# Large loads at one point of each twelve steps, masks made sooner, both halves of the maxima in one transposition, lists at every second step: a clustered-attention and mixture-of-experts kernel on one core

## The chip, the cores and the metric

The kernel runs on 1 core of one Trainium2 chip. TensorE multiplies matrices, VectorE (DVE), ScalarE (ACT) and GpSimd (POOL) work on the elements, and SyncE (SP) issues most of the copies (DMA). The metric is the device time of one execution, in microseconds (us); less is better. The time before is 1143.74 us, the median of three runs.

## The reference

Two stages follow each other. First an attention in which a query sees only the keys of its own cluster; then a layer of eight experts, of which each token uses the best two.

```python
# q, k, v: (4, 8, 768, 64); centroids: (8, 16, 64)
q_assign = argmax(einsum(q_n, c_n))          # cluster of each query; the same for k
mask = q_assign[:, :, :, None] == k_assign[:, :, None, :]
scores = where(mask, (q @ k.T) / sqrt(64), -1e9)
attn = softmax(scores, axis=-1)              # with 1e-9 added to the sum
x = (attn @ v), heads side by side           # (3072, 512)

noisy_logits = x @ w_gate + log1p(exp(x @ w_noise)) * noise      # 8 experts
top2, top2_w = the two largest, softmax over the two
for e in range(8):                           # w1: (8, 512, 1024), w2: (8, 1024, 512)
    out[mask] += top2_w * (relu(x[mask] @ w1[e]) @ w2[e])
```

## The kernel before, in words

**Precision.** Numbers are split into a high and a low half, so that the products come out in nearly fp32. `A` and `Bt` are the operands of the scores, three buffers each, used by the pair `p % 3`: high and low halves of q and k, a few rows for the mask (`A[64:80]`) and two rows for the negated row maxima (`Bt[96]`, `Bt[97]`), high and low.

**Steps.** Attention works on 16 pairs of heads (4 batches with 4 pairs each). A pair takes 12 steps, one for each of 2 heads x 6 blocks of 128 keys, so attention has 192 steps, with some in front and four behind. In step `t` the kernel issues, in this order: slot 0; `scores` of step `t`; `split_p` of step `t-1`; slot 1; `values` of step `t-4`; slot 2. Everything else is put into the slots by `at(step, function)`, where the fraction of the step (0, 1/3, 2/3) chooses the slot. The table `AT` holds these places. An engine works its own instructions in the order in which they were issued, and waits in that order; the engines are tied to each other only by what they need from each other. So SyncE, which computes nothing, may run far ahead of or behind the step in which a copy stands.

**What stands in the slots of a pair.** With w = 12(p-2) the preparation of pair p begins two pairs ahead:
- `load_qk` (two copies of 768 KB for four heads; one load in 24 steps) and `load_v` (768 KB, one in 24 steps, a single buffer `vt`, freed by `v_split`);
- `a_split` turns q and k and splits them into `hl`; `b_place` copies `hl` to `A` and `Bt` with ten copies on SyncE (`L434` to `L438`);
- `a_sims`, `a_sum`, `a_max1`, `a_ge`, `a_ky`, `a_max2`, `a_eq` find the cluster of each row on TensorE and VectorE and leave a one-hot `oh` (`L409`); `a_mask` transposes it on TensorE (`L418`) and ScalarE writes `mk`; `b_mask` copies `mk` to `A` with four copies on SyncE;
- `b_max` multiplies the masked scores for the maxima (`L454`), two matmuls a step for twelve steps, and VectorE reduces them (`L457`); it is the first to need the masks, at w + 9.333;
- `b_neg` joins the two halves of a row's maximum in `nm`; `b_negT` transposes `nm` (`L468`), makes the high part on ScalarE and the low part on VectorE, and sends each with a copy to `Bt`; the scores of the pair need them (the second matmul of `L485`).

`scores` makes two tiles a step, each of a matmul on `A` and one on `Bt`, and ScalarE takes their exponential into `pe`. `split_p` makes the low half `pl` of `pe` (`L496`) on GpSimd, for the last pair on VectorE. `values` multiplies high and low halves with v (`L513` to `L519`) and waits for `pl` at `L519`.

**Other work in the slots.** `zero_out` writes 512 KB of zeros to the output, twelve times; `zero_list` fills the table of the experts' tokens. After the last pair of a batch, `store_x` writes the batch's 1.5 MB, `g_logits` to `g_gate` choose the experts, and `g_list` writes the tokens' places into the table: 12 indirect copies a batch on GpSimd, each behind a small memset of `spacer` (`L701`, `L702`). Those of the last batch come after attention. `gather_x` fetches the rows of an expert's tokens; for the first expert's first four tiles it first clears `xg`. `load_w1` and `split_w1` of the first expert stand in the last ten steps.

**Experts.** Each expert has two layers of matmuls (`L952`, `L991`), 832 places an expert.

Of the kernel before, what the change touches and what calls it, by code (L numbers as in the profile page):

```python
# [9 lines left out]
F32 = mybir.dt.float32  # L10
F32R = mybir.dt.float32r
# [3 lines left out]
AF = mybir.ActivationFunctionType  # L15
OP = mybir.AluOpType
# [9 lines left out]
AT = dict(  # L26
    late=1,
    first={'place': -2.333, 'sims': [-3.333, -2.667], 'sum': [-2.333, -2.333], 'max1': -2.333, 'ge': -2.333, 'max2': -2.333, 'eq': -1.333, 'mask': 1.667, 'bmask': 4.0, 'ky': -2.333, 'split': [-5.333, -5.0, -5.333, -4.0], 'bmax': [10.0, 17.0], 'neg': [17.667, 24.667], 'negT': [20.667, 27.667]},
    L=4, qk=-15.667, v=-3.333,
    vscale=-0.667, vsplit=10.667, vstep=1.0, split=[-4.667, -3.667, -4.0, -3.333], place=-0.667,  # L30
    sims=[-3.0, 2.0], sum=[2.333, 3.333], max1=3.333, ge=3.667, max2=4.333, eq=4.667, mask=6.333, bmask=9.0,
    bmax=9.333, neg=20.333, negT=22.0, zero=19.667, zstep=4.333, store=2.667, log=1.667, log2=3.0,
    logstep=0.667, turn=7.667, list=24.0, lstep=1.0, bstep=1.0,
    gate=7.667, gstep=0.333, am=5.333, amstep=0.333, ky=4.0, cut=[13, 20], gplace=17.333,
    vd=[1, 1, 2, 3, 4, 5], sec=-7.333, qf=-13.667,
    fv={'v': -2.333, 'vscale': -1.0, 'am': 0.0, 'amstep': 0.333, 'vsplit': 3.0, 'vstep': 2.0},
    thr=0.333, bsec=0.0)

# [5 lines left out]
class Kernel:  # L44
# [116 lines left out]
    def attention(self, ctx):  # L161
        nc, tc = self.nc, self.tc
# [6 lines left out]
        self.A = [fix.tile([128, 2, 2, S], F32R, name=f"A{i}") for i in range(3)]  # L169
        self.Bt = [fix.tile([128, 2, 2, S], F32R, name=f"B{i}") for i in range(3)]  # L170
        self.oh = [fix.tile([128, 2, 3, 4, 32], BF, name=f"oh{i}") for i in range(2)]
        self.nm = fix.tile([128, 128], F32, name="nm")
        NP = B * H // 2
        self.NP = NP
        self.st = [dict() for _ in range(NP)]
        self.qk, self.vt, self.vv, self.am, self.xt, self.gx = {}, {}, {}, {}, {}, {}
        L = AT["L"]
        sched = {}

        def at(step, f, *a):  # L180
            sched.setdefault(divmod(round(3 * step), 3), []).append((f, a))

        def chain(step, by, fs):
            for i, f in enumerate(fs):
                at(step + by * i, f)


        T = AT
        for p in range(NP):
            b, hp = divmod(p, H // 2)  # L190
            w = 12 * (p - 2)
            if hp == 0:
                for g in range(2):
                    at(w + T["qk"] + 24 * g + (T["qf"] if (b, g) == (0, 1) else 0), self.load_qk, b, g)
                    v = w + 24 * g
                    V = T["fv"] if p + g == 0 else T
                    at(v + V["v"], self.load_v, b, g)
                    for h in range(0, 4, 2):
                        at(v + V["vscale"] + V["amstep"] * h, self.v_max, b, g, h)
                    chain(v + V["am"], V["amstep"], self.v_scale(b, g))  # L200
                    for h in range(4):
                        at(v + V["vsplit"] + V["vstep"] * h, self.v_split, b, g, h)
            P = T["first"] if p == 0 else T
            w += (0, T["sec"], T["thr"])[p] if p < 3 else 0
            for i in range(4):
                at(w + P["split"][i], self.a_split, p, i // 2, i % 2)
            if p == 0:
                at(w + P["sims"][0], self.c_turn)
            at(w + P["place"], self.b_place, p)
            for s in range(2):  # L210
                at(w + P["sims"][s], self.a_sims, p, s)
            for s in range(2):
                at(w + P["sum"][s], self.a_sum, p, s)
            for k, f in (("max1", self.a_max1), ("ge", self.a_ge), ("ky", self.a_ky), ("max2", self.a_max2),
                         ("eq", self.a_eq), ("mask", self.a_mask), ("bmask", self.b_mask)):
                at(w + P[k], f, p)
            if p == 0:
                for s in range(2):
                    for j in range(NJ):
                        at(w + P["bmax"][s] + j, self.b_max, p, s, j)  # L220
                    at(w + P["neg"][s], self.b_neg, p, s, 1)
                    at(w + P["negT"][s], self.b_negT, p, s, 1)
            else:
                w = 12 * (p - 2) + (T["bsec"] if p == 1 else 0)
                for s in range(2):
                    for j in range(NJ):
                        at(w + T["bmax"] + T["bstep"] * (6 * s + j), self.b_max, p, s, j)
                at(w + T["neg"], self.b_neg, p, 0, 2)
                at(w + T["negT"], self.b_negT, p, 0, 2)
            if hp == H // 2 - 1:  # L230
                z = w + 36 + L
                if b + 1 == B:
                    continue
                at(z + T["store"], self.store_x, b)
                for jj in range(NJ):
                    at(z + T["log"] + T["logstep"] * jj, self.g_logits, b, jj)
                    at(z + T["log2"] + T["logstep"] * jj, self.g_logits2, b, jj)
                at(z + T["turn"], self.g_turn, b)
                fs = self.g_gate(b)
                chain(z + T["gate"], T["gstep"], fs[:self.GP])  # L240
                chain(z + T["gplace"], T["gstep"], fs[self.GP:])
                for j in range(2 * NJ):
                    at(z + T["list"] + T["lstep"] * j, self.g_list, b, j)
        at(T["zero"] - 4, self.zero_list)
        for i in range(self.N // 256):
            at(T["zero"] + T["zstep"] * i, self.zero_out, i)
        z = 12 * NP
# [6 lines left out]
            at(z - 7 + i, self.gather_x, 0, i)  # L254
        for i in range(2):
            nc.gpsimd.memset(self.oh[i], 0.0)
        nc.gpsimd.memset(self.nm, 0.0)
        self.fixed_init(0)
        at(-14.4, self.fixed_init, 1)
        at(-8.4, self.fixed_init, 2)  # L260
        self.at = at
        for t in range(min(sched)[0], z + L + 2):
            u = t - L
            slot = lambda i: [f(*a) for f, a in sched.pop((t, i), [])]
# [6 lines left out]
            if 0 <= u < z:  # L271
                p, s, kc = u // 12, (u % 12) // 6, u % 6
# [185 lines left out]

    def b_neg(self, p, s, n):

        W, c = n * self.NJ, self.NJ * s
        self.nc.vector.tensor_tensor(self.nm[:, 0:W], self.aux[:, 500 + c:500 + c + W], self.st[p]["mm"][:, c:c + W],
                                     op=OP.min)

    def b_negT(self, p, s, n):
        nc, W = self.nc, n * self.NJ
        t = self.ps()
        nc.tensor.transpose(t[:, :128], self.nm, self.ident)  # L468
        t = t[:W, :128]
        hi, lo = (self.wk.tile([16, 128], F32R, name=f"nt{i}") for i in range(2))  # L470
        nc.scalar.activation(hi[:W], t, AF.Copy)
        nc.vector.tensor_tensor(lo[:W], t, hi[:W], op=OP.subtract)
        for i, x in enumerate((hi, lo)):
            self.dma(self.Bt[p % 3][96 + i:97 + i, 1, s:s + n], x[:W])


    def scores(self, p, s, kc):
# [11 lines left out]
    def split_p(self, p, s, kc):  # L489

        nc, st = self.nc, self.st[p]
        pe = st["p", s, kc].rearrange("p a n -> p (a n)")
        hi = pe.bitcast(BF).rearrange("p (n two) -> p n two", two=2)[:, :, 1]
        lo = self.wk.tile([128, self.S], F16, name="pl", bufs=5)

        (nc.vector if p == self.NP - 1 else nc.gpsimd).tensor_tensor(lo, pe, hi, op=OP.subtract)  # L496
        st["p", s, kc] = hi, lo

    def values(self, p, s, kc):
# [424 lines left out]
    def gather_x(self, e, t):  # L924
        xg = self.mw.tile([128, self.DM], F32, name="xg", bufs=4)
        r = self.rows(t)
        first = e == 0 and t < self.TA
        n = self.N - self.S if first else self.N
        if first:
            self.nc.gpsimd.memset(xg, 0.0)  # L930
        self.nc.gpsimd.indirect_dma_start(  # L931
            out=xg[:r], out_offset=None, in_=self.xs[:n],
            in_offset=bass.IndirectOffsetOnAxis(ap=self.entry(e, t)[:r, 0:1], axis=0),
            bounds_check=n - 1, oob_is_err=False)
        self.xg[e, t] = xg
# [117 lines left out]
```

## Time and profile before

| what | value |
|---|---|
| runs | 1143.74 us median, 1143.65 to 1147.19 |
| profiled execution | 1145.87 us, of which the span is 1144.0 us |
| busy: TensorE | 1072.6 us, 94% |
| busy: VectorE | 603.8 us, 53% |
| busy: GpSimd | 571.5 us, 50% |
| busy: ScalarE | 479.4 us, 42% |
| HBM | 78.21 MB read, 26.53 MB written |
| TensorE busy, 100 to 500 us | 90.13, 93.76, 95.83, 90.69 us in each 100 us |
| TensorE busy, 700 to 900 us | 200.00 us of 200 us |

The span reaches from the first to the last instruction; the rest of the execution's time lies around it. The first scores start at 50.06 us and attention ends at about 510 us; after that come the experts. "Busy" counts a matmul from its start to its modelled end. In the lists of waits the engine before the arrow waits and the one behind it released it; `ring` is the group of six PSUM buffers that nearly all matmuls write. SPq is SyncE's queue of issued copies.

### The profile page before, as it was taken

Reading aid. Unit: us, or ns where it says so; the run is one execution under the profiler, and the core shown is the slowest. Engines: PE = TensorE matmul, PEld = TensorE weight load, DVE = VectorE, ACT = ScalarE, POOL = GpSimd, SP = SyncE. Lnnn points to the kernel's source line nnn. Section 1 sums busy time; section 2 is a strip of 40 time slices with the busy share of each in tenths; the row PEclk is TensorE's granted clock in tenths of the full one; section 3 lists DMA queues with packets and bytes.
Section 4 is the critical chain, followed back from the end, with each engine's and each line's share of the span. In section 5 each row is a group of like instructions: output and inputs, shape, how many; then the busy total and the mean of one; then the engine's idle time right before and its main releaser. Section 6 shows DMA issues by size and latency. Waiting matters only on the chain. (4 is left out here: it accounts for less than half of the span.)

```text
span 1144.0 us, 22354 instructions
## 1 busy us (share of the span) xinstructions
PE 1072.6 (94%) x8658; PEld 950.4 (83%) x8658; DVE 603.8 (53%) x1298; ACT 479.4 (42%) x961; POOL 571.5 (50%) x619
## 2 busy tenths in 40 slices
PE   4898889999999999989899999999999999999995
PEld 4588787888888888878799889899898898998984
DVE  5876675776688667676145424433344244433411
ACT  3475656666676667564043313223133132231300
POOL 4776664789578957863444323342343233512311
PEclk7899999998999999989899999999999999999998
DMA  8866777664755554122336224432353143423200
GB/s 226 182 151 144 186 179 205 161 152 114 201 120 147 119 147 92 58 91 95 99 95 225 84 72 164 131 109 91 125 171 99 65 150 130 130 86 119 74 31 31
DMA packets 87677, 144.46 MB, mean 126 GB/s; under 512 B 14295, under 2 KB 65879, under 8 KB 87056
## 3 DMA queue, kind: packets, MB, share of 16 engines
q1 hardware_dynamic: 72272, 106.45, 35.0%
q0 software_dynamic: 13712, 36.42, 9.5%
q8 instruction: 69, 1.13, 0.4%
q10 hardware_dynamic: 1584, 0.13, 0.1%
q14 instruction: 40, 0.33, 0.1%
HBM read 78.21 MB, written 26.53 MB: 92 GB/s over the span
## 5 line engine op out<-in xcount | busy, mean ns | idle before, releaser
L496 POOL TENSOR_TENSOR pl<-pe 128x768 f16<-128x768 f32 x180 | 263.3, 1472 | 99.2 <-ACT pe L486 90.3
L952 PE MATMUL ring<-xT,w1t 128*128 128x416 f32 (+2 forms) x1536 | 290.3, 350 | 0.0
L952 PEld LDWEIGHTS ring<-xT,w1t 128*128 128x128 f32 x1536 | 282.7, 188 | 6.6 <-DVE xT L905 0.3
L991 PE MATMUL ring<-w2t,hT 128*128 128x512 f32 x1152 | 273.7, 394 | 0.0
L991 PEld LDWEIGHTS ring<-w2t,hT 128*128 128x128 f32 x1152 | 214.5, 189 | 43.3
L486 ACT ACTIVATE pe<-ring,l 128x384 f32<-128x384 f32 x384 | 202.0, 578 | 93.2 <-PE ring L485 83.6
L1004 POOL DMA_INDIRECT out<-yo,lst x56 | 65.6, 1172 | 236.8 <-DVE yo L1000 187.4
L457 DVE TENSOR_REDUCE aux<-ring 128x1 f32<-128x384 f32 x192 | 107.8, 561 | 94.4 <-PE ring L454 89.9
L485 PE MATMUL ring<-A 128*128 128x384 f32 x384 | 144.3, 376 | 1.0 <-DVE aux L457 0.5
L485 PE MATMUL ring<-B 128*128 128x384 f32 x384 | 132.7, 346 | 4.2 <-DMA B<-nt 4.0
L961 ACT ACTIVATE hT<-ring 128x416 fp32r<-128x416 f32 (+3 forms) x128 | 56.7, 488 | 180.6 <-PE ring L952 168.5
L962 DVE SCALAR_TENSOR_TENSOR hT<-ring,hT 128x416 fp32r<-128x416 f32 (+3 forms) x128 | 66.2, 554 | 123.9 <-ACT hT L961 122.8
L454 PE MATMUL ring<-A 128*128 128x384 f32 x384 | 114.7, 373 | 17.1 <-DMA A<-mk 8.6
L931 POOL DMA_INDIRECT xg<-xs,lst x56 | 65.7, 1173 | 128.5 <-PE ring L942 105.1
L1000 DVE SCALAR_TENSOR_TENSOR yo<-ring,lst,xt 128x512 f32<-128x512 f32 (+1 forms) x49 | 36.7, 750 | 166.6 <-PE ring L991 146.1
L457 DVE TENSOR_REDUCE mm<-ring 128x1 f32<-128x384 f32 x192 | 105.0, 547 | 0.1
L904 ACT ACTIVATE xT<-ring 128x512 fp32r<-128x512 f32 (+1 forms) x56 | 31.0, 566 | 173.1 <-PE ring L942 172.8
L454 PEld LDWEIGHTS ring<-A 128*128 128x128 f32 x384 | 71.5, 197 | 34.6 <-ACT pe L486 14.6
L513 PE MATMUL av<-vv,pe 128*128 128x65 f16 x1152 | 98.9, 196 | 1.1 <-DVE xt L527 1.1
L515 PE MATMUL av<-vv,pe 128*128 128x64 f16 x1152 | 98.0, 194 | 0.0
L513 PEld LDWEIGHTS <-pe 128*128 128x128 bf16 x1152 | 81.7, 100 | 14.8 <-issue 10.9
L485 PEld LDWEIGHTS ring<-B 128*128 128x128 f32 x384 | 74.7, 195 | 6.7 <-issue 4.4
(173 smaller groups left out, 1360.3 us busy)
## 6 DMA issues: line engine op xcount, KB each, us to landing
stg<-in_moe_w SPq DMA_DIRECT2D x64, 512.0 KB
A<-hl SPq DMA_DIRECT2D x30, 384.0 KB
B<-hl SPq DMA_DIRECT2D x30, 384.0 KB
vt<-in_v SPq DMA_DIRECT2D x8, 768.0 KB
out<-zt SPq DMA_DIRECT2D x12, 512.0 KB
xs<-xt SPq DMA_DIRECT2D x4, 1536.0 KB
A<-hl SPq DMA_DIRECT2D x60, 96.0 KB
B<-hl SPq DMA_DIRECT2D x30, 192.0 KB
```

The costliest lines, as they stand in the source:

```text
L454: nc.tensor.matmul(t, A[:, 0, s, j * 128:j * 128 + 128], A[:, 1, s, n * 384:n * 384 + 384], start=True, stop=True)
L457: nc.vector.tensor_reduce(o, t, axis=X, op=OP.max, negate=True)
L485: nc.tensor.matmul(t, M[:, 1 - qi, s, ks], M[:, qi, s, ns], start=not qi, stop=bool(qi))
L486: nc.scalar.activation(pe[:, n], t, AF.Exp, bias=self.l64[:, 0:1], scale=self.scale)
L496: (nc.vector if p == self.NP - 1 else nc.gpsimd).tensor_tensor(lo, pe, hi, op=OP.subtract)
L513: nc.tensor.matmul(av[:, j, :], ph[:, js], vv[:, hh, kj, 64:129], start=(kc == 0 and j == 0), stop=False, skip_group_check=True)
L515: nc.tensor.matmul(av[:, j, :64], ph[:, js], vv[:, hh, kj, 0:64], start=False, stop=False, skip_group_check=True)
L931: self.nc.gpsimd.indirect_dma_start(out=xg[:r], out_offset=None, in_=self.xs[:n], in_offset=bass.IndirectOffsetOnAxis(ap=self.entry(e, t)[ ...
L952: nc.tensor.matmul(p, self.w1t[:, wi, c, f * 128:f * 128 + 128], self.xT[:, xi, c, n0:n1], start=(i == 0), stop=(i == 3 * ND - 1))
L962: nc.vector.scalar_tensor_tensor(h1, x, 0.0, h0, op0=OP.max, op1=OP.subtract)
L991: nc.tensor.matmul(p, self.hT[:, hi, f, t * 128:t * 128 + 128], self.w2t[:, wi, f], start=(i == 0), stop=(i == 3 * NF - 1))
L1004: i = nc.gpsimd.indirect_dma_start(out=self.out, out_offset=bass.IndirectOffsetOnAxis(ap=en[:r, 0:1], axis=0), in_=yo[:r], in_offset=None, ...
```

## The change

- `load_qk` moves from w - 15.667 to w - 20.667 (for the second load at the start, `qf` keeps its place), `load_v` from v - 3.333 to v - 8.667 (the first keeps its place), and `zero_out` from every 4.333 steps from step 19.667 on to every 12 steps from step 27 on. So these copies stand at steps 3 to 3.333 of each twelve. `zero_list` keeps its place (15.667) under a name of its own.
- `a_mask` moves from w + 6.333 to w + 5.667 and `b_mask` from w + 9 to w + 6. The first pair has its own table and keeps its places.
- `b_neg` now makes the low and the high half of the maxima itself, beside each other in `nm`; `b_negT` transposes both at once, with one ScalarE copy and one DMA behind it.
- `g_list` is put at every second step for batches 0 and 1, from step 23 after the batch's mark instead of 24; batch 2 keeps one a step and starts one step sooner.
- From step 5 of the last pair but one, `split_p` is on VectorE (before: only in the last pair).
- The four memsets of `xg` go from GpSimd to VectorE.

```diff
-    L=4, qk=-15.667, v=-3.333,
+    L=4, qk=-20.667, v=-8.667,
 ...
-    sims=..., eq=4.667, mask=6.333, bmask=9.0,
-    bmax=9.333, neg=20.333, negT=22.0, zero=19.667, zstep=4.333, store=2.667, ...
-    logstep=0.667, turn=7.667, list=24.0, lstep=1.0, bstep=1.0,
+    sims=..., eq=4.667, mask=5.667, bmask=6.0,
+    bmax=9.333, neg=20.333, negT=22.0, zero=27.0, zstep=12.0, zlist=15.667, store=2.667, ...
+    logstep=0.667, turn=7.667, list=23.0, lstep=[2.0, 2.0, 1.0], bstep=1.0,
 ...
-    vd=[1, 1, 2, 3, 4, 5], sec=-7.333, qf=-13.667,
+    vd=[1, 1, 2, 3, 4, 5], sec=-7.333, qf=-8.667,
 ...
-                    at(z + T["list"] + T["lstep"] * j, self.g_list, b, j)
-        at(T["zero"] - 4, self.zero_list)
+                    at(z + T["list"] + T["lstep"][b] * j, self.g_list, b, j)
+        at(T["zlist"], self.zero_list)
 ...
     def b_neg(self, p, s, n):
-        W, c = n * self.NJ, self.NJ * s
-        self.nc.vector.tensor_tensor(self.nm[:, 0:W], self.aux[:, 500 + c:500 + c + W], self.st[p]["mm"][:, c:c + W],
-                                     op=OP.min)
+        v, W, c = self.nc.vector, n * self.NJ, self.NJ * s
+        o = self.aux[:, 500 + c:500 + c + W]
+        hi, lo = (self.nm[:, W * i:W * i + W] for i in range(2))
+        v.tensor_tensor(o, o, self.st[p]["mm"][:, c:c + W], op=OP.min)
+        v.tensor_copy(hi, o)
+        v.tensor_tensor(lo, o, hi, op=OP.subtract)
     def b_negT(self, p, s, n):
-        nc, W = self.nc, n * self.NJ
+        nc, W = self.nc, 2 * n * self.NJ
         t = self.ps()
-        nc.tensor.transpose(t[:, :128], self.nm, self.ident)
-        t = t[:W, :128]
-        hi, lo = (self.wk.tile([16, 128], F32R, name=f"nt{i}") for i in range(2))
-        nc.scalar.activation(hi[:W], t, AF.Copy)
-        nc.vector.tensor_tensor(lo[:W], t, hi[:W], op=OP.subtract)
-        for i, x in enumerate((hi, lo)):
-            self.dma(self.Bt[p % 3][96 + i:97 + i, 1, s:s + n], x[:W])
+        nc.tensor.transpose(t[:, :128], self.nm.bitcast(F32), self.ident)
+        nt = self.wk.tile([32, 128], F32R, name="nt")
+        nc.scalar.activation(nt[:W], t[:W, :128], AF.Copy)
+        self.dma(self.Bt[p % 3][96:98, 1, s:s + n], nt[:W])
 ...
-        (nc.vector if p == self.NP - 1 else nc.gpsimd).tensor_tensor(lo, pe, hi, op=OP.subtract)
+        last = p == self.NP - 1 or (p == self.NP - 2 and 6 * s + kc >= 5)
+        (nc.vector if last else nc.gpsimd).tensor_tensor(lo, pe, hi, op=OP.subtract)
 ...
-            self.nc.gpsimd.memset(xg, 0.0)
+            self.nc.vector.memset(xg, 0.0)
```

More of the change, by code (lines that the diff above doesn't have):

```diff
@@ L28 @@
     first={'place': -2.333, 'sims': [-3.333, -2.667], 'sum': [-2.333, -2.333], 'max1': -2.333, 'ge': -2.333, 'max2': -2.333, 'eq': -1.333, 'mask': 1.667, 'bmask': 4.0, 'ky': -2.333, 'split': [-5.333, -5.0, -5.333, -4.0], 'bmax': [10.0, 17.0], 'neg': [17.667, 24.667], 'negT': [20.667, 27.667]},
-    L=4, qk=-15.667, v=-3.333,
+    L=4, qk=-20.667, v=-8.667,
     vscale=-0.667, vsplit=10.667, vstep=1.0, split=[-4.667, -3.667, -4.0, -3.333], place=-0.667,
-    sims=[-3.0, 2.0], sum=[2.333, 3.333], max1=3.333, ge=3.667, max2=4.333, eq=4.667, mask=6.333, bmask=9.0,
-    bmax=9.333, neg=20.333, negT=22.0, zero=19.667, zstep=4.333, store=2.667, log=1.667, log2=3.0,
-    logstep=0.667, turn=7.667, list=24.0, lstep=1.0, bstep=1.0,
+    sims=[-3.0, 2.0], sum=[2.333, 3.333], max1=3.333, ge=3.667, max2=4.333, eq=4.667, mask=5.667, bmask=6.0,
+    bmax=9.333, neg=20.333, negT=22.0, zero=27.0, zstep=12.0, zlist=15.667, store=2.667, log=1.667, log2=3.0,
+    logstep=0.667, turn=7.667, list=23.0, lstep=[2.0, 2.0, 1.0], bstep=1.0,
     gate=7.667, gstep=0.333, am=5.333, amstep=0.333, ky=4.0, cut=[13, 20], gplace=17.333,
-    vd=[1, 1, 2, 3, 4, 5], sec=-7.333, qf=-13.667,
+    vd=[1, 1, 2, 3, 4, 5], sec=-7.333, qf=-8.667,
     fv={'v': -2.333, 'vscale': -1.0, 'am': 0.0, 'amstep': 0.333, 'vsplit': 3.0, 'vstep': 2.0},
@@ L171, in attention @@
         self.oh = [fix.tile([128, 2, 3, 4, 32], BF, name=f"oh{i}") for i in range(2)]
-        self.nm = fix.tile([128, 128], F32, name="nm")
+        self.nm = fix.tile([128, 128], F32R, name="nm")
         NP = B * H // 2
@@ L256, in attention @@
             nc.gpsimd.memset(self.oh[i], 0.0)
-        nc.gpsimd.memset(self.nm, 0.0)
+        nc.gpsimd.memset(self.nm.bitcast(F32), 0.0)
         self.fixed_init(0)
```

## The prediction

> **What bounds the kernel now.** I read the page's first part, then the engine waits of TensorE in the attention stage, then the windows and the timelines around those waits.
>
> ```profile
> span 1144.0 us, 22354 instructions
> PE 1072.6 (94%) x8658; PEld 950.4 (83%) x8658; DVE 603.8 (53%) x1298; ACT 479.4 (42%) x961; POOL 571.5 (50%) x619
> ```
>
> The engine waits of TensorE, 90 to 520 us (columns: total, times, longest):
>
> ```profile
> PE av L519 <- POOL spacer L701: 10.3, 7, 2.3
> PE ring L454 <- DMA A<-mk: 8.6, 4, 3.1
> PE ring L485 <- DMA B<-nt: 3.7, 4, 1.6
> PE ring L454 <- issue: 2.8, 1, 2.8
> ```
>
> TensorE is busy for 94% of the span, so a microsecond in which it stands still in attention is a microsecond of the result; work that other engines lose is not. The waits name three causes. `L519` waits for `pl`, which GpSimd makes late when it also writes the lists (10.3 us). `L454` waits for the masks' copy into `A` (8.6 us in four gaps, and a fifth of 2.8 us that the trace calls "issue" but that lies at the same place). `L485` waits for the maxima in `B` (3.7 us). Together 25.4 us.
>
> TensorE's timeline at three gaps (idle time before the row in brackets), and windows of 10 us:
>
> ```profile
> 130.59 0.96 PE L454 MATMUL ring<-A 128*128 128x384 f32 x2 [3.10 <-DMA A<-mk]
> 271.04 0.51 PE L519 MATMUL av<-vv,pl 128*128 128x65 f16 x6 [2.33 <-POOL spacer L701]
> 388.17 0.35 PE L519 MATMUL av<-vv,pl 128*128 128x65 f16 x6 [2.00 <-POOL spacer L701]
> ```
>
> ```profile
> 100.00:110.00 10.00, 9.93 (x121) 9.17 (x122) 7.96 (x17) 4.52 (x9) 4.88 (x4) 0.83 0.38 78
> 130.00:140.00 10.00, 9.41 (x118) 8.64 (x119) 5.97 (x15) 6.61 (x14) 4.32 (x5) 0.83 0.33 69
> 270.00:280.00 10.00, 8.96 (x76) 8.33 (x77) 3.61 (x8) 5.03 (x9) 9.80 (x9) 0.66 0.34 97
> 390.00:400.00 10.00, 10.00 (x117) 9.75 (x117) 6.05 (x14) 6.85 (x14) 9.75 (x8) 0.83 0.11 20
> 490.00:500.00 10.00, 7.78 (x83) 7.04 (x84) 7.55 (x11) 5.65 (x9) 7.14 (x11) 0.66 0.19 55
> ```
>
> The five windows are those of attention in which the granted clock (third number from the right) drops, and each begins in or just behind a gap of 2 us or more. A mean of 0.83 over 10 us is worth 1.7 us of full-speed work, 0.66 is worth 3.4: up to 11.9 us more hang on the gaps.
>
> The Trainium skill, page "TensorE: Matmul & The Clock Gate", section "HAM oscillation — how this bites in real kernels", sets its limit at idle gaps above about 3.4 us. The trace does not agree: its gap of 2.00 us at 388.17 is followed by a drop. By the page's limit no gap here would cost clock.
>
> **The change part by part.** *Loads and masks.* The masks' copies wait in the one SyncE queue behind the loads, not for their step:
>
> ```profile
> 104.46 2.97 SPq L426 DMA_DIRECT2D A<-hl  x3
> ...
> 115.00 2.69 SPq L555 DMA_DIRECT2D out<-zt  x2
> 117.73 1.58 SPq L293 DMA_DIRECT2D qk<-in_q  x1
> 119.36 1.45 SPq L293 DMA_DIRECT2D qk<-in_k  x1
> 120.85 1.19 SPq L555 DMA_DIRECT2D out<-zt  x1
> 122.15 4.73 SPq L426 DMA_DIRECT2D A<-mk  x4
> ```
>
> ```profile
> 126.00:128.00 2.00, 1.49 (x9) 1.17 (x8) 1.05 (x3) 1.47 (x4) 0.90 (x1) 1.00 1.11 363
> 128.00:130.00 2.00, 0.00 (x0) 0.00 (x0) 0.00 (x0) 0.57 (x2) 1.29 (x1) 1.00 0.48 139
> ```
>
> The ten placing copies (`L434` to `L438`) hold SyncE from 104.46 to 115.00, then three zeroings (512 KB each) and q and k (768 KB each) go out, then the masks; the queue runs dry at about 129 and the matmul starts at 130.59. After the change only one zeroing stands in each twelve steps, so two of three go: 2.6 us less issuing and 1 MB less, at the 363 GB/s of the last full window some 3 us, so the masks land near 126.5. TensorE stopped at 127.5 (130.59 less 3.10). In the periods of the other gaps one or two zeroings, or the store of `xt`, leave the queue ahead of the masks in the same way. In the period before 100 us one zeroing goes, but a load of v and the zeroed list stay; I leave 0.4 us there. Of 11.4 us idle 11.0 go, and of the clock behind the first two (1.7 each, ends 0 and 3.4) I take 2.4, since part of a slow window lies in the gap itself: **-13.4**. The zeroings now come later, in eight periods that had none; 0.5 MB is 1.5 us there, in front of masks that TensorE did not wait for. I take nothing; if that cover is gone it is 1 us in three periods. The load of v now stands 1.7 steps behind the last split that frees its buffer (7 before), but SyncE reaches it later still, after the ten copies: nothing; where GpSimd is late with that split, the masks would wait behind it.
>
> *The masks sooner.* The transposition `L418` moves from just behind the first scores of step 6 to the end of step 5. It needs `oh`, and VectorE is late with it:
>
> ```profile
> 88.53 0.42 PE L485 MATMUL ring<-A 128*128 128x384 f32 x1
> ...
> 88.63 0.56 DVE L409 TENSOR_TENSOR oh<-ring,km 128x384 bf16<-128x384 f32 x1
> ...
> 448.86 0.42 PE L485 MATMUL ring<-A 128*128 128x384 f32 x1
> ...
> 449.39 0.56 DVE L409 TENSOR_TENSOR oh<-ring,km 128x384 bf16<-128x384 f32 x1
> ```
>
> These are the first and the last of thirteen pairs: the first score of step 6, and the `oh` that would have to be done before it. In the first `oh` ends 0.66 us after that score's start (89.19 to 88.53), in the last 1.09. Eight of the thirteen are late by 0.44 to 1.09, three are early by 0.2, and two were covered by the `pl` gaps, which go, and would then be late by about 0.6. Ten waits of 0.8 with 0.07 for the signal: **+8.6**. Behind the waiting `L418` stand all later scores. Ends: 0, if shorter waits behind it (for `pe`, for ring buffers) shrink as much, and 14 x 1.1 = 15. No wait of this size lowered the clock: the smallest gap with a drop is 2.00.
>
> *One transposition of both halves.* `b_neg` gets two more small VectorE operations; `b_negT` loses one VectorE operation and one copy of two, so the maxima land about 1 us sooner. Of 3.7 us, longest 1.6, I take **-3.2** (ends 0 and 3.7), and +0.5 for the longer VectorE part in front of the transposition and of `places`, which reads after it.
>
> *q and k sooner, at the start.* For the second batch the load moves ahead of the second maxima of the first pair on SyncE:
>
> ```profile
> 58.67 1.71 SPq L426 DMA_DIRECT2D B<-nt  x2
> 60.48 0.39 SPq L293 DMA_DIRECT2D qk<-in_q  x1
> 60.93 0.49 SPq L293 DMA_DIRECT2D qk<-in_k  x1
> ...
> 63.44 0.33 PE L485 MATMUL ring<-B 128*128 128x384 f32 x1
> ```
>
> The matmul at 63.44 uses these maxima, without a wait now. With 1.5 MB ahead of them, 4 to 5 us at that rate, they land at 65 to 67: **+2.5** (ends 0 and 5). The Trainium skill, "DMA: Bandwidth & Descriptors", section "Queues, rings and completion order", says that each DMA engine takes the descriptors of a ring in order; the masks behind the loads above agree.
>
> *Lists at every second step.*
>
> ```profile
> 470.07 1.48 POOL L496 TENSOR_TENSOR pl<-pe 128x768 f16<-128x768 f32 x1
> ...
> 471.75 0.99 POOL L702 DMA_INDIRECT tbl<-rec,pk  x1 [0.17 <-issue]
> 472.76 1.48 POOL L496 TENSOR_TENSOR pl<-pe 128x768 f16<-128x768 f32 x1
> ...
> 473.51 0.42 PE L485 MATMUL ring<-A 128*128 128x384 f32 x1
> 475.21 0.42 PE L485 MATMUL ring<-A 128*128 128x384 f32 x1
> ```
>
> With a list in each step GpSimd needs 2.69 us per step (470.07 to 472.76); a light step of TensorE takes 1.70. At every second step it is (2.69 + 1.48)/2 = 2.1 on average. Over whole pairs a step takes 2.5 (448.86 - 88.53 = 360.3 us for twelve pairs), of which the gaps are 0.2: GpSimd just keeps up, and values run four steps behind the scores. So the two gaps of batches 0 and 1 go: 2.33 + 2.00 = 4.3, and of their clock (3.4 + 1.7) I take 4.4: **-8.7** (ends 4 and 9.4).
>
> The third batch keeps a list per step, but the last seven splits of the last pair but one go to VectorE:
>
> ```profile
> 510.54 1.51 PE L942 MATMUL ring<-ident,xg 128*128 128x128 f32 x12
> ```
>
> ```profile
> L496 DVE TENSOR_TENSOR pl<-pe 128x768 f16<-128x768 f32 x12 | 12.4, 1063 | 5.3 <-ACT pe L486 5.3
> ...
> L457 DVE TENSOR_REDUCE aux<-ring 128x1 f32<-128x384 f32 x192 | 107.8, 561 | 94.4 <-PE ring L454 89.9
> ...
> L905 DVE TENSOR_TENSOR w1t<-stg,w1t 128x1024 fp32r<-128x1024 f32 x32 | 37.8, 1218 | 3.4 <-ACT w1t L904 3.4
> ...
> L930 POOL MEMSET xg<- 128x512 f32 x4 | 2.2, 546 | 0.0
> ```
>
> The five remaining `pl` gaps (10.3 - 4.3 = 6.0) and the clock of the last window (up to 3.4) lie there, but VectorE becomes the bound. From the first moved split (at 470, the row above) to the end of attention (510.54, where `L942` transposes the gathered rows) stand 40.5 us. VectorE's work there will be 19 splits x 1.06 = 20.2, 8 reductions x 0.56 = 4.5, four weight halves x 1.22 = 4.9, four outputs of pairs (three small operations each, estimated as two reductions) 4.5, four memsets at most 0.55 = 2.2, 0.6 of small work: 36.9, and some 10% less where they overlap. So 3.6 to 7.3 go; I take **-5.0**.
>
> Everything behind attention keeps its length. Sum: -13.4 - 3.2 - 8.7 - 5.0 + 8.6 + 2.5 + 0.5 = -18.7. The profiled execution took 1145.87, so 1127.2; the median of the runs, 1143.74, is 2.1 lower, which gives **1125.0**.
>
> **The rivals.** *The wait for `oh` costs nothing.* TensorE's short waits behind it shrink by as much: 1116. Against it: the late `oh` is in eight pairs already.
>
> *The masks land late still.* They remain behind the placing copies, one zeroing and one big load, and my margins are 1 to 2 us. If 8 of the 13.4 stay it is 1133, and with the later zeroings at 1 us in three periods 1136.
>
> *The clock does not hang on gaps of 2 us.* Then 2.4 + 4.4 stay: 1132. Against it: all five drops stand at such gaps. It is the page's limit on idle gaps that would make it so.
>
> *Slower.* `L418` stops TensorE in every pair, and from 2.0 us on each stop lowers the clock too: fourteen times 2.0 and half of 1.7 is 40, against 27 that the rest brings: 1156. It decides from 2.2 us a pair with no clock loss; the latest `oh` is 1.09 late, so VectorE would have to lose another microsecond in each pair, and the new `b_neg` operations (0.17 like the one there) don't give that.
>
> **How the numbers follow.** Forecast 0.55, with a range of its own of 1117 to 1134; no cost of `oh` 0.16; late masks 0.17; clock 0.05; slower 0.07. A tenth below 1112 and a tenth above 1137 are left out. A measurement tells 0.3%, 3.4 us, from no change. Below 1140.3 lie all cases but the slower one and the worst of the late masks: 0.86 faster, 0.07 same, 0.07 slower.
>
> **What would show it.** In the waits of TensorE: `A<-mk` and "issue" at `L454` under 1 us; `L519 <- POOL` none; a new `L418 <- DVE oh` of 6 to 10 us in about ten times; `L485 <- B<-nt` one wait of 2 to 3 us near 63 us and little else. Granted clock 1.00 in all windows from 100 to 480. VectorE nearly without idle time in the last 35 us of attention, which ends near 492 instead of 510.5. Wrong if `L418` waits 2 us, if `A<-mk` stays above 5 us, or if the time saved in attention is lost again before the first expert matmuls.

## The result, and the profile after

The changed kernel takes 1116.9 us (median of six runs, 1115.96 to 1117.97) beside 1145.57 before (six runs, with new ones beside the change): ratio 0.9749, 95% interval 0.9732 to 0.9766, 28.7 us less. The prediction was 18.7 us less, 1125.0, with a range of 1112 to 1137. Measured once more, in the last set below, the same kernel was 20 us faster than the kernel before (ratio 0.9825): the size of the gain is known to some 9 us, its direction is clear in both.

The page of the changed kernel:

```profile
span 1114.9 us, 22318 instructions
PE 1056.4 (95%) x8658; PEld 943.2 (85%) x8658; DVE 612.7 (55%) x1326; ACT 476.8 (43%) x961; POOL 559.2 (50%) x608
```

The waits of TensorE in its attention, 90 to 490 us, the stretch in which the clock had dropped four times before, and the one window of attention in which it drops now (granted clock third from the right):

```profile
PE ring L418 <- DVE oh L409: 6.0, 10, 1.0
PE av L514 <- DVE xt L528: 4.4, 2, 3.4
PE ring L454 <- DMA A<-mk: 1.8, 2, 1.0
PE ring L454 <- ACT pe L486: 1.5, 6, 0.3
PE ring L471 <- DVE nm L466: 1.3, 1, 1.3
...
60.00:480.00 420.00, 399.89 (x5304) 363.14 (x5303) 327.44 (x806) 291.03 (x594) 314.55 (x287) 1.00 0.60 151
470.00:480.00 10.00, 6.58 (x105) 6.10 (x105) 9.33 (x15) 4.43 (x9) 4.44 (x6) 0.85 0.37 107
```

The three causes named before have gone or nearly so: the waits for `pl` (10.3 us) and for the maxima (3.7) have no row any more, and of 11.4 us for the masks 1.8 are left. The ten waits for `oh` are the new ones that were forecast. The four drops of the clock between 60 and 480 us went with their gaps: the mean is 1.00 over 420 us. At the end of attention one drop is left, 0.85 over 10 us behind the new wait of 3.4 us for `xt`; before, 0.66 stood there. TensorE's timeline shows the maxima late at the start, one of the waits for `oh`, and one of the two masks that still come late:

```profile
65.76 0.45 PE L485 MATMUL ring<-B 128*128 128x384 f32 x1 [1.46 <-DMA B<-nt]
...
125.53 0.59 PE L454 MATMUL ring<-A 128*128 128x384 f32 x2 [0.97 <-DMA A<-mk]
...
201.13 0.51 PE L418 MATMUL ring<-identb,oh 128*128 128x128 bf16 x6 [0.95 <-DVE oh L409]
```

### The profile page after: what moved, and what is told of

It reads as the page before. It is cut to its first block, busy times and chain, and to the rows that moved or that the text cites. A ratio compares the mean times of both kernels' runs of the same rounds, so it can differ in the third digit from the quotient of the medians.

```text
span 1114.9 us, 22318 instructions
## 1 busy us (share of the span) xinstructions
PE 1056.4 (95%) x8658; PEld 943.2 (85%) x8658; DVE 612.7 (55%) x1326; ACT 476.8 (43%) x961; POOL 559.2 (50%) x608
## 5 line engine op out<-in xcount | busy, mean ns | idle before, releaser
L497 POOL TENSOR_TENSOR pl<-pe 128x768 f16<-128x768 f32 x173 | 252.2, 1473 | 72.3 <-ACT pe L486 69.5
L485 PE MATMUL ring<-A 128*128 128x384 f32 x384 | 141.3, 368 | 0.3 <-DVE aux L457 0.3
L485 PE MATMUL ring<-B 128*128 128x384 f32 x384 | 129.4, 337 | 1.8 <-DMA B<-nt 1.8
L454 PE MATMUL ring<-A 128*128 128x384 f32 x384 | 110.5, 363 | 7.5 <-ACT pe L486 2.6
L514 PE MATMUL av<-vv,pe 128*128 128x65 f16 x1152 | 98.2, 196 | 4.5 <-DVE xt L528 4.4
L514 PEld LDWEIGHTS <-pe 128*128 128x128 bf16 x1152 | 80.5, 99 | 19.9 <-issue 11.8
L454 PEld LDWEIGHTS ring<-A 128*128 128x128 f32 x384 | 71.0, 194 | 20.3 <-ACT pe L486 9.8
L516 PEld LDWEIGHTS <-pe 128*128 128x128 bf16 x1152 | 78.8, 99 | 0.3
```

The source lines that it names most:

```text
L454: nc.tensor.matmul(t, A[:, 0, s, j * 128:j * 128 + 128], A[:, 1, s, n * 384:n * 384 + 384], start=True, stop=True)
L485: nc.tensor.matmul(t, M[:, 1 - qi, s, ks], M[:, qi, s, ns], start=not qi, stop=bool(qi))
L497: (nc.vector if last else nc.gpsimd).tensor_tensor(lo, pe, hi, op=OP.subtract)
L514: nc.tensor.matmul(av[:, j, :], ph[:, js], vv[:, hh, kj, 64:129], start=(kc == 0 and j == 0), stop=False, skip_group_check=True)
L516: nc.tensor.matmul(av[:, j, :64], ph[:, js], vv[:, hh, kj, 0:64], start=False, stop=False, skip_group_check=True)
```

## Experiments

All ratios are to the kernel before, run beside them in the same set. Runs of one set share a chip; between sets the ratio of one kernel moved by up to 0.8% (the last set), so kernels are compared within a set, and across sets by their traces.

### First set: single parts

**mask_back**: the changed kernel with the transposition back in step 6.

```diff
-    mask=5.667, bmask=6.0,
+    mask=6.333, bmask=6.333,
```

> The changed kernel (1116.9 us) with the masks' transposition back behind the first scores of step 6 and their copies right behind it; all else of the change stays. Theory A (the prediction: each wait of L418 for oh is paid in full): the waits of 6.0 us in attention go, about 1111. Theory B (the wait is only a shift: steps 5 and 6 together were as long before, because TensorE waited in step 6 for ring buffers held up by ScalarE's mk): 1116 to 1118, with L454 <- ACT pe back at some 3 to 4 us and L418 <- oh gone. Theory C (the sooner masks are needed): A<-mk waits grow by 3 us or more, 1120.

Measured: 1115.18 us, ratio 0.9769 (0.9749 to 0.9788). Its waits of TensorE, 90 to 520 us:

```profile
PE ring L454 <- ACT pe L486: 5.2, 18, 0.4
...
PE ring L454 <- DMA A<-mk: 0.2, 1, 0.2
```

Theory B. The 6.0 us for `oh` are gone, and the short waits for `pe` grow from 1.5 us in six times to 5.2 in eighteen. The first scores of steps 5, 6 and 7 of the fourth pair, before, changed, and in this run, say where they lie; the first two show the matmuls for the maxima in step 6 as well:

```profile
146.32 0.33 PE L485 MATMUL ring<-A 128*128 128x384 f32 x1
...
148.96 0.42 PE L485 MATMUL ring<-A 128*128 128x384 f32 x1
...
150.28 0.44 PE L454 MATMUL ring<-A 128*128 128x384 f32 x1 [0.21 <-ACT pe L486]
...
151.45 0.42 PE L485 MATMUL ring<-A 128*128 128x384 f32 x1
```

```profile
139.69 0.33 PE L485 MATMUL ring<-A 128*128 128x384 f32 x1
...
143.33 0.42 PE L485 MATMUL ring<-A 128*128 128x384 f32 x1
...
144.11 0.52 PE L454 MATMUL ring<-A 128*128 128x384 f32 x2
...
145.03 0.42 PE L485 MATMUL ring<-A 128*128 128x384 f32 x1
```

```profile
138.76 0.33 PE L485 MATMUL ring<-A 128*128 128x384 f32 x1
...
141.39 0.42 PE L485 MATMUL ring<-A 128*128 128x384 f32 x1
...
143.89 0.42 PE L485 MATMUL ring<-A 128*128 128x384 f32 x1
```

Step 5 grows from 2.64 us to 3.64 and step 6 shrinks from 2.49 to 1.70: together 5.13 before, 5.34 changed, 5.13 here. Some 0.3 us of the shift is the transposition itself, which moved from step 6 to step 5. The rest of step 6's gain, some 0.5 us, is the wait of its second `L454` for `pe` (listed with 0.21, since idle time counts from the modelled end of a matmul); in the changed kernel ScalarE has released the buffer by then. So of a wait listed with 0.52 us in this pair 0.21 is paid.

**masks_alone**: the kernel before with the masks' two places alone.

```diff
-    mask=6.333, bmask=9.0,
+    mask=5.667, bmask=6.0,
```

> The kernel before (1145.6 us) with only the masks' two places changed. Theory A (waits for oh paid in full): 6 to 8 us longer, 1152 to 1154. Theory B (a shift): 1144 to 1147, L418 <- oh of 6 to 8 us and as much less elsewhere in step 6. Theory C (masks sooner on SyncE shorten the A<-mk gaps by themselves, since their copies now stand ahead of q, k, v and the zeroings of the same twelve steps): 5 to 12 us shorter, 1134 to 1141.

Measured: 1130.71 us, ratio 0.9902 (0.9884 to 0.9920), 11 us less. Theory C. In the waits of 90 to 520 us there is no row for `A<-mk` at all; these are the longest:

```profile
PE av L519 <- POOL spacer L701: 9.1, 6, 2.8
PE ring L485 <- DMA B<-nt: 5.7, 6, 1.6
PE ring L418 <- DVE oh L409: 4.7, 7, 1.0
```

SyncE's queue of this run shows why; these are the copies that stood in the opposite order in the prediction's rows:

```profile
111.31 2.65 SPq L555 DMA_DIRECT2D out<-zt  x2
116.41 2.61 SPq L426 DMA_DIRECT2D A<-mk  x4
119.06 0.59 SPq L293 DMA_DIRECT2D qk<-in_q  x1
119.70 0.56 SPq L293 DMA_DIRECT2D qk<-in_k  x1
120.30 0.60 SPq L555 DMA_DIRECT2D out<-zt  x1
```

SyncE waits 2.45 us for `mk` (113.96 to 116.41), and the loads wait behind the masks instead of the masks behind the loads.

**loads_alone**: the kernel before with only the places of the loads, the zeroings and the zeroed list.

```diff
-    L=4, qk=-15.667, v=-3.333,   zero=19.667, zstep=4.333,               qf=-13.667
+    L=4, qk=-20.667, v=-8.667,   zero=27.0, zstep=12.0, zlist=15.667,    qf=-8.667
```

> The kernel before with only the places of the loads of q, k, v, the zeroings and the zeroed list changed; the masks' copies keep their place at step 9. By the prediction's terms: A<-mk 13.4 us less, B<-nt at 63 us 2.5 more: 1134.7. If the masks' copies had to be sooner too, half of the gaps stay: 1139 to 1141.

Measured: 1133.76 us, ratio 0.9912 (0.9886 to 0.9938), some 10 us less, as the prediction's terms had it; the rival's 1139 to 1141 lies outside the interval. The agreement is partly luck: by this run's trace the first pair is 6.2 us longer (31.76 us beside 25.53), not 2.5, and the stretch from the first score of the second pair to that of the fifteenth 16.6 us shorter (369.30 beside 385.85), not 13.4. The waits for the masks fall from 11.4 to 3.3 us in two times, and in 50 to 90 us TensorE waits for the maxima behind q and k:

```profile
PE ring L454 <- DMA A<-mk: 3.3, 2, 2.1
...
PE ring L485 <- DMA B<-nt: 3.8, 3, 3.3
```

So each of two edits removes most of the same gaps, and their gains can't be added.

**lists_alone**: the kernel before with the lists at every second step, the seven more splits and the four memsets on VectorE.

```diff
-    list=24.0, lstep=1.0,
+    list=23.0, lstep=[2.0, 2.0, 1.0],
-        (nc.vector if p == self.NP - 1 else nc.gpsimd).tensor_tensor(lo, pe, hi, op=OP.subtract)
+        last = p == self.NP - 1 or (p == self.NP - 2 and 6 * s + kc >= 5)
+        (nc.vector if last else nc.gpsimd).tensor_tensor(lo, pe, hi, op=OP.subtract)
-            self.nc.gpsimd.memset(xg, 0.0)
+            self.nc.vector.memset(xg, 0.0)
```

> The kernel before with only the lists at every second step, seven more splits on VectorE and the four memsets on VectorE. By the prediction's terms 8.7 + 5.0 us less: 1131.9. By the lengths of the pairs in the trace after (two pairs shorter by about 5 and 4, the last pair and the tail by 3.3): 1133. If VectorE were not the bound of the last stretch: 9 + 9 less, 1127.

Measured: 1131.39 us, ratio 0.9906 (0.9883 to 0.9929), 11 us less. As ratios to the 1145.6 us that they start from, the forecasts are 0.988 (the terms), 0.989 (the pairs' lengths) and 0.984 (VectorE not the bound): the second lies in the interval (0.9883 to 0.9929), the first just under it, the third well outside. Its waits agree: `pl` has no row left, and `L514 <- DVE xt` stands at 3.9 us, 3.4 of it at the end of attention.

### Second set

**no_loads**: the changed kernel with the loads, zeroings and the zeroed list at their old places (the `loads_alone` edit backwards).

> The changed kernel with the loads, the zeroings and the zeroed list back at the places they had before; masks, maxima and lists stay changed. Theory A (the loads had to be gathered for the masks to land in time, as the prediction's largest term says): A<-mk gaps come back, 5 us or more longer than the changed kernel. Theory B (the masks' sooner place on SyncE does that by itself; the gathered loads only cost the wait near 65 us and the two remaining A<-mk waits): 3 to 5 us shorter than the changed kernel, ratio to before about 0.971, the first pair 25.5 us instead of 28.1.

Measured: 1111.89 us, ratio 0.9732 (0.9709 to 0.9755). Theory B by the trace: no row for `A<-mk` in its waits, and the first pair takes 26.07 us where the changed kernel takes 28.14. The ratio is 2 us under the changed kernel's 0.9749, less than the 3 to 5 expected, and as the two come from different sets the runs alone don't show a gain. Gathering the loads isn't needed once the masks' copies stand ahead of them.

**qk_later**: the changed kernel with q and k of the second batch behind the first pair's second maxima.

```diff
-  (T["qf"] if (b, g) == (0, 1) else 0)
+  (T["qf"] if (b, g) == (0, 1) else 1.0 if (b, g) == (1, 0) else 0)
```

> The changed kernel with one load moved: q and k of the second batch's first half go out one step later, behind the second maxima of the first pair on SyncE. If these maxima are late because 1.5 MB stand ahead of them: the wait of 1.5 us at 65.8 goes and the first pair is 1 to 2.6 us shorter, so 1 to 3 us shorter than the changed kernel. If something else makes the first pair 2.6 us longer (the load of v, the masks), no difference.

Measured: 1116.77 us, ratio 0.9777 (0.9752 to 0.9801), no less than the changed kernel's 0.9749 in its own set. In the trace the wait at 65.8 us is gone and the first pair takes 26.08 us instead of 28.14; the time of the runs doesn't resolve 2 us across two sets. So the wait's cause is shown by the trace, its price by the pair's length only.

**tail_shared**: the changed kernel with every second split of the last pair on GpSimd.

```diff
-        last = p == self.NP - 1 or (p == self.NP - 2 and 6 * s + kc >= 5)
+        n = 6 * s + kc
+        last = (p == self.NP - 1 and n % 2 == 0) or (p == self.NP - 2 and n >= 5)
```

> The changed kernel with every second split of the last pair on GpSimd instead of VectorE (six of twelve). Theory A (VectorE's work is what bounds the last stretch): the waits of 4.4 us for xt and part of 1.3 us for nm go, 3 to 5 us shorter. Theory B (a two-input operation of VectorE on SBUF stands still while GpSimd runs one: at 445.97 and 448.64 us two splits took 1.81 and 2.33 us beside a split on GpSimd instead of 0.94): six times up to 1.48 us lost for 5.5 us of work taken away, so between 1 us shorter and 3 us longer.

Measured: 1117.02 us, ratio 0.9791 (0.9768 to 0.9814): nothing gained. The largest of its waits of 440 to 485 us:

```profile
PE av L521 <- POOL pl L498: 4.0, 2, 3.3
```

The 4.4 us for `xt` became 4.0 for `pl`: GpSimd's splits stand behind the gathers of `xg`, which wait in turn for VectorE (2.49 us in front of the first). That VectorE's amount of work bounds the stretch is neither shown nor refuted by this run; the order on GpSimd took its place.

**neg_alone**: the kernel before with only the new `b_neg` and `b_negT`.

> The kernel before with only both halves of the maxima in one transposition. By the prediction's term: B<-nt waits of 3.7 us fall to 0.5 us, 2.7 us shorter in all (ratio 0.9975). Rival: the one copy spreads over no more engines than each of the two and lands no sooner than the second one did: no difference.

Measured: 1136.12 us, ratio 0.9949 (0.9930 to 0.9967), 5.8 us less, twice the term. The waits for `B<-nt` behind 90 us are all gone, and those for the masks fell as well, without an edit there:

```profile
PE av L519 <- POOL spacer L701: 11.9, 7, 2.8
PE ring L454 <- DMA A<-mk: 6.6, 2, 3.5
PE ring L454 <- ACT pe L486: 5.0, 17, 0.4
```

Each period's first copy on SyncE is that of the maxima, and the ten placing copies and the masks stand behind it. In the third pair's period the first copy of the masks follows that of the maxima after 18.74 us, beside 19.50 before; yet this period's gap is as long as it was (3.11 us beside 3.10). So why the masks' waits fell from 11.4 to 6.6 us, in two gaps instead of five, isn't shown.

### Third set

**after_again** is the changed kernel once more, **tail_lists** the kernel of no_loads with the third batch's lists later and the memsets on GpSimd, **no_loads_mask_back** that of no_loads with the masks of mask_back.

```diff
 tail_lists:
-    list=23.0, lstep=[2.0, 2.0, 1.0],
+    list=[23.0, 23.0, 26.0], lstep=[2.0, 2.0, 0.667],
-            self.nc.vector.memset(xg, 0.0)
+            self.nc.gpsimd.memset(xg, 0.0)
```

> The changed kernel itself, beside the two below on the same chip: ratio to before 0.975.

> The changed kernel with the loads at their old places, the third batch's lists three steps later and closer together (step 26 on, two thirds of a step apart), and the memsets of xg on GpSimd again. If VectorE bounds the last stretch and loses 2.3 us there to splits that stand beside those of GpSimd, GpSimd's splits are done sooner and VectorE has 1.9 us less work: the waits of 1.3 (nm) and 3.4 us (xt) shrink, 2 to 3.5 us shorter than the changed kernel with the old loads alone (which was 0.973 of before), so 0.971. If the lists now come too late for the first gathers: no gain or a wait at the first transposition of xg.

> The changed kernel with the loads at their old places and the masks' transposition behind the first scores of step 6 again, their copies right behind it and still ahead of the loads on SyncE. If what counts is the place of the masks' copies on SyncE and not that of the transposition: no A<-mk wait and the same time as with the old loads alone, 0.972 to 0.974, with L418 <- oh gone and L454 <- ACT pe at 4 to 5 us instead of 1.5. If the transposition's sooner place matters: A<-mk waits of 3 us or more.

Measured: after_again 1122.47 us, ratio 0.9825 (0.9798 to 0.9853); tail_lists 1113.0, 0.9744 (0.9717 to 0.9771); no_loads_mask_back 1119.92, 0.9811 (0.9783 to 0.9838). All three are slower than expected: 0.975, 0.971, and 0.972 to 0.974. All three lose 5 to 7 us in the first six steps of the last pair (14.16, 16.01 and 15.00 us; 9.17 in the changed kernel's first profile), to short waits that the trace calls "issue" and a stretch of lower clock behind them. after_again loses 2.6 us in the first pair as well (30.71 us beside 28.14): its wait for the maxima there is 2.84 us, beside 1.46, and 3.4 us at half clock follow it. Here is the changed kernel's window at the start of the last pair in the first profile and in this one:

```profile
457.00:467.00 10.00, 8.98 (x153) 8.02 (x150) 8.31 (x13) 8.91 (x16) 5.58 (x9) 1.00 0.20 56
```

```profile
461.00:471.00 10.00, 7.97 (x81) 6.39 (x77) 3.48 (x4) 4.02 (x8) 5.49 (x9) 0.67 0.02 2
```

What TensorE waits for there no view of the trace names, so it stays open. Within the set tail_lists is 9.5 us faster than the changed kernel (its upper interval end, 0.9771 of before, lies under that kernel's lower one, 0.9798). By the traces 4.6 us of this are in the first pair, where the old places of the loads count, and 3.7 from the first score of the last pair but one to the first gathered transposition: the waits for `nm` are gone and those for `xt` fell to 1.5 us, beside 4.4 us in no_loads. It beats the kernel before and the changed one; that it beats no_loads (0.9732 in the second set) isn't shown. no_loads_mask_back again has no row for `A<-mk`, `L454 <- ACT pe` 4.7 us and no `L418 <- DVE oh` behind 90 us: for the masks' waits the place of their copies on SyncE is what counts, not that of the transposition. Its time was not the same, though. From the first score of the second pair to that of the fifteenth it takes 360.89 us, beside 357.50 in tail_lists and 356.58 in no_loads, and waits 3.5 us for `B<-nt` where no_loads waits 0.5. So with the loads at their old places the later transposition, with the copies behind it, costs some 3 to 4 us there; why was not tried.

## Why the prediction was right or wrong

- **Direction and mechanisms held.** The three named waits went, the forecast new ones came at the forecast places: `L418 <- oh` ten times (6.0 us, 6 to 10 forecast), one wait for the maxima near 63 us (1.46 at 65.76, 2 to 3 forecast), `xt` at the end of attention. Not as forecast: `A<-mk` is 1.8 us, not under 1; VectorE stands idle for 4.4 of its last 35 us; the clock is 0.85 from 470 to 480 us. The measured 1116.9 lies just under the forecast's own range, 1117 to 1134.
- **The step that failed is the price of the waits for `oh`, +8.6.** I took every wait of TensorE as paid. The waits are there, but TensorE had waited in step 6 already, for `pe` (mask_back), and those waits shrank. The traces price it from the first score of the second pair to that of the fifteenth, which contain nothing of either end of attention; changed kernel, then mask_back:

```profile
77.62 0.42 PE L485 MATMUL ring<-A 128*128 128x384 f32 x1
...
435.91 0.42 PE L485 MATMUL ring<-A 128*128 128x384 f32 x1
```

```profile
77.47 0.42 PE L485 MATMUL ring<-A 128*128 128x384 f32 x1
...
434.18 0.42 PE L485 MATMUL ring<-A 128*128 128x384 f32 x1
```

  358.29 against 356.71: 1.6 us, and the difference of their `A<-mk` waits (1.8 to 0.2) is as much. So beside the gathered loads the term was between 0 and 1.6, near its lower end; the same stretch of the changed kernel in the third set, 358.79, says the same. The rival "the wait for `oh` costs nothing", 1116, is the case that came, 1116.9, with a chance of 0.16 given to it. A row of before could have told that part of the wait would be taken out of others, in TensorE's waits from 90 to 520 us; with `L418` moved it fell to 1.5 us in six:

```profile
PE ring L454 <- ACT pe L486: 4.0, 15, 0.4
```

- **Loads and masks, -13.4, was near in size, and credited to one of two edits that each do it.** The gaps went but for 1.8 us. I gave all to the zeroings and loads that leave the queue, and looked at the masks' sooner place only as a cost. The masks' place alone brings 11 us, the loads' places alone 10; those besides cost the maxima at the start.
- **q and k sooner, +2.5:** the first pair grew from 25.53 to 28.14 us, 2.6, of which 2.1 go with the place of q and k (qk_later, 26.08). The order on SyncE was read rightly; that the size fits is partly luck, for the same edit made the first pair 27.13 us in tail_shared, 30.71 in after_again and 31.76 in loads_alone.
- **Lists at every second step, -8.7:** the two pairs with the gaps fell from 30.65 to 25.52 and from 29.71 to 25.52 us, 9.3.
- **The last stretch, -5.0:** from the first score of the last pair but one to the first gathered transposition 49.1 us before (461.44 to 510.54) and 45.8 after:

```profile
435.91 0.42 PE L485 MATMUL ring<-A 128*128 128x384 f32 x1
...
481.75 1.51 PE L943 MATMUL ring<-ident,xg 128*128 128x128 f32 x12
```

  3.3 less. VectorE lost 2.3 us that were not costed, in the splits told of below. That the sum of VectorE's work bounds this stretch isn't shown (tail_shared).
- **One transposition, -3.2 + 0.5:** 5.8 alone, with a part of the masks' gaps in it.
- **The clock, -6.8 in two terms:** the four drops it stands for are gone, but what they cost wasn't measured apart from their gaps. The reading given with it, that the clock drops at gaps from 2 us on and that all five drops of before stand at such gaps, does not hold. No gap of 2 us stands at the fifth drop (490 to 500 us), where the longest is 1.66; and a gap of 2.31 us at 193.61 has a clock of 1.00 all around it:

```profile
193.61 0.63 PE L454 MATMUL ring<-A 128*128 128x384 f32 x2 [2.31 <-DMA A<-mk]
...
493.74 0.51 PE L519 MATMUL av<-vv,pl 128*128 128x65 f16 x6 [1.66 <-POOL spacer L701]
```

With the term for `oh` at 0, its lower end, the sum would be 18.7 + 8.6 = 27.3 less, beside 28.7 measured. That they are so near is partly luck. The spans differ by 29.1 us (1144.0 and 1114.9): 0.6 in front of the first scores, 27.6 between the first scores of the second and the fifteenth pair (9.3 of it the lists), 3.3 in the last stretch and 0.3 behind it are gained, 2.6 in the first pair lost. So 18.2 us fall to masks, loads, maxima, clock and `oh` together, where the terms, with `oh` at 0, give 13.4 + 3.2 - 0.5 = 16.1; the 2 us between them have no cause shown. And in after_again, where the kernel gained 20 us, that middle stretch was the same to 0.5 us; its time came near the forecast of 18.7 by losses in the first and the last pair that the forecast had not named.

## What to carry to other kernels

Where copies share a queue, the first question is what stands ahead of the one that somebody waits for: putting the small urgent copy in front of the loads did as much as thinning and regrouping the loads, and did not bring the wait at the start that these brought. A new wait of the bottleneck engine is paid only as far as it isn't taken out of waits that it already has close behind; look for those rows before adding its full length. Two edits that remove the same gap must not be summed.

## What the runs showed of the hardware that was not expected

VectorE's split took twice its time when GpSimd ran one at the same time. VectorE's and then GpSimd's timeline of the changed kernel:

```profile
445.97 1.81 DVE L497 TENSOR_TENSOR pl<-pe 128x768 f16<-128x768 f32 x1
...
448.64 2.33 DVE L497 TENSOR_TENSOR pl<-pe 128x768 f16<-128x768 f32 x1
...
451.82 0.94 DVE L497 TENSOR_TENSOR pl<-pe 128x768 f16<-128x768 f32 x1
```

```profile
445.48 1.48 POOL L497 TENSOR_TENSOR pl<-pe 128x768 f16<-128x768 f32 x1
...
448.66 1.48 POOL L497 TENSOR_TENSOR pl<-pe 128x768 f16<-128x768 f32 x1
```

GpSimd's end at 446.96 and 450.14 plus 0.8 us each is where VectorE's two end (447.78, 450.97): VectorE stood still for the rest of GpSimd's operation, and GpSimd kept its 1.48 us. The third split, beside no such operation, took 0.94. In all nine kernels with splits moved to VectorE, each of VectorE's 18 splits that overlap one of GpSimd's ends 0.80 to 0.83 us behind it. The Trainium skill, page "SBUF — State Buffer", section "SBUF: two separate sides", calls the pair of ports that VectorE and GpSimd share an exclusive lock: a VectorE operation with two SBUF inputs contends for it with a GpSimd operation that reads SBUF, and whichever starts first has it for the whole instruction. The trace agrees, except that at 448.64 VectorE's start is shown 0.02 us ahead of GpSimd's and it was still VectorE that waited.

The granted clock fell without a long gap, too. In tail_lists no gap of TensorE between 452 and 463 us is over 0.52 us, but it was busy for about half of the time; windows of 2 us (TensorE's busy time behind the first comma, the clock third from the right):

```profile
456.00:458.00 2.00, 1.15 (x10) 0.87 (x10) 0.02 (x1) 0.00 (x0) 1.78 (x3) 1.00 0.02 1
458.00:460.00 2.00, 0.90 (x15) 0.58 (x14) 0.03 (x1) 1.16 (x2) 1.56 (x5) 1.00 0.02 1
460.00:462.00 2.00, 0.90 (x5) 0.64 (x6) 0.93 (x1) 0.00 (x0) 1.77 (x4) 0.71 0.02 1
462.00:464.00 2.00, 1.74 (x8) 0.78 (x8) 0.00 (x0) 0.90 (x2) 0.45 (x1) 0.50 0.01 1
```

With the drop behind a gap of 2.00 us in the kernel before, none behind its gap of 2.31 us, and one among gaps of at most 1.66 us, this speaks for a share of busy time over a few microseconds as what counts, rather than the length of a single gap; no run here tried it by itself.
